# Loading keys a pair ahead of values in a single-core attention-decode kernel

## The chip, the core and the metric

The kernel runs on one core of one Trainium2 chip. The metric is the device time of one execution in microseconds (us): the median of three runs. TensorE (PE) multiplies matrices, VectorE (DVE) and ScalarE (ACT) do elementwise work, SyncE (SP) issues nearly all loads, and sixteen DMA engines carry them out.

## The reference

One new token attends to a cache of 65,536 tokens, with 16 query heads of width 256 that share 8 key/value heads in twos; a small mixer over the 448 model channels is blended in by a gate.

```python
g = sigmoid((x * gate_w).sum(-1))                 # x: 1 x 1 x 448
q = (x @ wq) as 16 heads of 256                   # k_cache, v_cache: 8 heads x 65536 x 256, bf16
scores = q . k * 256**-0.5                        # query heads 2g, 2g+1 use key/value head g
a = (softmax(scores) @ v) as one row of 4096 @ wo # 448 channels
h = layernorm(x)
b = gelu(h * w1 + b1) @ w2 + b2                   # per channel, through 1792 hidden units
out = g * a + (1 - g) * b
```

The two caches hold 537 MB, all of which is read once.

## The kernel before, in words

The work is cut into `NP` = 32 *pairs*, four (`PPH`) to each of `H` = 8 key/value heads. A pair is 16,384 cache rows: 128 rows (`NV`) of 256 values on each of 128 partitions, 8.39 MB of keys and as much of values. Its keys go through TensorE in eight chunks (`BODY`) of 16 rows (`NT`).

**Buffers.** `vbuf` holds the value rows of one pair. `kring` holds 192 rows: keys of an even pair stand in rows 0 to 127, those of an odd pair in rows 64 to 191. Both kinds of pair use the middle, rows 64 to 127, and every pair transposes the middle first (`tiles(HV)`, chunks 0 to 3), then its own side (`tiles(0)` or `tiles(NV)`). So the next pair's keys can be loaded when half of this pair's chunks are transposed.

**One pair on TensorE.** `keys`: each chunk is transposed into PSUM (`kst`, line 334); VectorE evacuates two of the four banks to `ktT` (line 616) and ScalarE the other two (line 751); then the scores against the two current queries `qcur` follow (line 353), one chunk behind the transposes. `values`: first `maxima`, a round trip in which VectorE reduces the scores (line 622), TensorE transposes (374) and spreads (376) the maximum, ScalarE makes the factor `fade` and the weights `pT` (734, 738), and VectorE scales the running sums in `acc` (645). Then TensorE adds the denominators (392) and multiplies the 128 value rows (403). In the first 14 pairs (`FT`), VectorE also does one step of the mixer after the maxima (`mixer`, lines 585 to 610) and TensorE adds its product (513).

**After four pairs**, the head ends: VectorE copies the sums (`take`, 650), TensorE clears `acc` and turns the head's output over partitions (`by_row`), VectorE scales it (676) and sets the next head's `qcur` (669), and TensorE projects it with this head's `wo` (450). The last head ends in `tail()`.

**The order of loads** is written out by hand in the SP queue: for each pair j, wait until half of pair j-1 is transposed, load keys j; wait until values j-1 are multiplied (`sem_pv`), load values j; once a head, wait for the projection and load the next `wo`. Everything else waits on the semaphores that these loads raise. Keys of pair 30 come in halves, of pair 31 in quarters, and the values of pair 31 as rows 0 to 95, 96 to 111, 112 to 123 and 124 to 127 (`pieces`), followed by the last head's `wo` in two halves. `spin` (line 369) multiplies without use, eight times before the last values and once in the tail.

Of the kernel before, what the change touches and what calls it, by code (L numbers as in the profile page):

```python
# [12 lines left out]
def bass_gated_mix__gqa_block_cached__mixer_token_mlp__decode_kernel(  # L13
# [17 lines left out]
    H = A_k_cache.shape[1]  # L31
# [4 lines left out]
    REP = HQ // H  # L36
# [27 lines left out]
    NFIRST = 96  # L64
    NLATE = 112
    pieces = [(NFIRST, NLATE), (NLATE, 124), (124, NV)]
# [16 lines left out]
    QV = NV // 4  # L83
# [10 lines left out]
    with ctx:  # L94
# [101 lines left out]
        sem_kp = new_sem("sem_kp")  # L196
        sem_kq = [new_sem("sem_kq%d" % i) for i in range(3)]
# [53 lines left out]
        @block.sync  # L251
        def _(eng):
            def load_wo(g):
                w = A_wo[g * REP * DH:(g + 1) * REP * DH, :]
                eng.dma_start(wo_rows, w.rearrange("(p i) n -> p (i n)", i=2 * REP)).then_inc(sem_wo, 16)

            load_wo(0)
            eng.dma_start(wq_a.rearrange("p j n -> p (j n)"),
                          A_wq[0:WF * P, :].rearrange("(p j) n -> p (j n)", p=P)).then_inc(sem_wq, 16)
            eng.dma_start(wq_b, A_wq[WF * P:DM, :].rearrange("r (a n) -> (r a) n", a=2)  # L260
                          ).then_inc(sem_wq, 16)
            def load(dst, cache, j, n0, n1, at, sem):
                eng.dma_start(dst[:, at + n0:at + n1, :].rearrange("p n d -> p (n d)"), src(cache, j, n0, n1)
                              ).then_inc(sem, 16)

            for j in range(NP):
                last = j == NP - 1
                if j >= 1:
                    eng.wait_ge(sem_tr[NB - 1], BODY * (j - 1) + DC)
                if j == 0:  # L270
                    load(kring, A_k_cache, j, HV, NV, 0, sem_k)
                    load(kring, A_k_cache, j, 0, HV, 0, sem_kb)
                elif last:
                    for i, sem in enumerate([sem_k] + sem_kq):
                        load(kring, A_k_cache, j, i * QV, (i + 1) * QV, HV, sem)
                elif j == NP - 2:
                    load(kring, A_k_cache, j, HV, NV, 0, sem_k)
                    load(kring, A_k_cache, j, 0, HV, 0, sem_kp)
                else:
                    load(kring, A_k_cache, j, 0, NV, HV * (j % 2), sem_k)  # L280
# [5 lines left out]
                load(vbuf, A_v_cache, j, 0, NFIRST if last else NV, 0, sem_v)  # L286
                if last:
                    for (n0, n1), sem in zip(pieces, sem_vp):
                        load(vbuf, A_v_cache, j, n0, n1, 0, sem)
                g, m = divmod(j, PPH)  # L290
                if m == 0 and 1 <= g < H - 1:
                    eng.wait_ge(s_proj, g)
                    load_wo(g)

            eng.wait_ge(s_proj, H - 1)
            for h in range(REP):
                w = A_wo[(HQ - REP + h) * DH:(HQ - REP + h + 1) * DH, :]
                eng.dma_start(wo_sb[:, h, :], w.rearrange("(p j) n -> p (j n)", j=2)).then_inc(sem_wl[h], 16)
            eng.wait_ge(s_fin, NCG)
            eng.dma_start(out_ap, out_row[:, :]).then_inc(sem_out, 16)  # L300
            eng.wait_ge(sem_out, 16)
# [13 lines left out]
        def _(pe):  # L315
# [3 lines left out]
            def transposes(k, c, j, u16, x2):  # L319
                if k == 0:  # L320
                    pe.wait_ge(sem_k, u16)
                if k == DC:
                    pe.wait_ge(sem_kb, 16)
                    with pe.If(j == NP - 2):
                        pe.wait_ge(sem_kp, 16)
                if k and k % (DC // 2) == 0:
                    with pe.If(j == NP - 1):
                        pe.wait_ge(sem_kq[k // (DC // 2) - 1], 16)
# [17 lines left out]
            def scores(k, c):  # L346
                par = k % 2
                for nt in range(NT):
# [10 lines left out]
            def keys(c0, *where):  # L359
                transposes(0, c0, *where)  # L360
                for k in range(1, BODY):
                    transposes(k, c0 + k, *where)
                    scores(k - 1, c0 + k - 1)
                scores(BODY - 1, c0 + BODY - 1)


            def spin(n):
                for _ in range(n):
                    pe.matmul(kst[:, NB - 1, :], ones_sq[:, :], ktT[:, KTB - 1, 0, 0:512], start=True, stop=True)  # L369
# [9 lines left out]
            def values(j, c0, u16):  # L379
                j1 = pe.snap(j + 1, min_val=1, max_val=NP)  # L380
                maxima(j1)
                with pe.If(j == NP - 1):
                    pe.wait_ge(s_mix, 1)
                    for q in range(NCG):
                        r = slice(32 * q, 32 * q + 1)
                        pe.matmul(prj[r, 0:WG], rest[r, :], brow[r, :], start=False, stop=True,
                                  skip_group_check=True)
                    spin(8)
                pe.wait_ge(s_acc, j1)
                pe.wait_ge(sem_exp, j1)  # L390
# [4 lines left out]
                def some(n0, n1, last=False):  # L395
                    if last:
                        piece_wait(n0)
                    else:
                        pe.wait_ge(sem_v, u16)
                    for n in range(n0, n1):  # L400
                        r, nt = divmod(n, NT)
                        o = 32 * (n % 4)
                        ins = pe.matmul(acc[o:o + REP, 0:DH], pT[:, r, 2 * nt:2 * nt + 2], vbuf[:, n, :],  # L403
                                        start=False, stop=False, skip_group_check=True)
                    return ins

                some(0, NFIRST)
                with pe.If(j < NP - 1):
                    some(NFIRST, NV).then_inc(sem_pv, 1)
                with pe.Else():  # L410
                    some(NFIRST, NLATE, last=True).then_inc(s_early, 1)
                    tail()
# [43 lines left out]
            def tail():  # L456
# [3 lines left out]
                spin(1)  # L460
# [40 lines left out]
            pe.reg_mov(x2_reg, 0)  # L501
            on = OrderedEngineSet([pe.engine])
            with nc.Fori(0, H, 1, engines=on, head_slot={pe.engine: 0}) as g:
                with nc.Fori(0, PPH, 1, engines=on, head_slot={pe.engine: 0}) as m:
                    j = pe.snap(g * PPH + m, min_val=0, max_val=NP - 1)
# [3 lines left out]
                    values(j, c0, u16)  # L509
                    with pe.If(j < FT):  # L510
                        pe.wait_ge(s_pb, j + 1)
# [3 lines left out]
                    pe.reg_sub(x2_reg, NV, x2_reg)  # L515
                with pe.If(g < H - 1):
                    pe.wait_ge(s_cp, g + 1)
                    clear(acc[:, 0:NACC])
                    by_row(acc[:, SELC:NACC]).then_inc(s_sel, 1)
                    pe.wait_ge(sem_wo, pe.snap(g * 16 + 16, min_val=16, max_val=16 * H))  # L520
                    pe.wait_ge(s_oTn, g + 1)
                    project(range(2 * REP)).then_inc(s_proj, 1)

        @block.vector
        def _(vec):
# [140 lines left out]
            def finish_head(g):  # L666
                take(vec.snap(g * PPH + PPH, min_val=PPH, max_val=NP))
                vec.memset(mrun[:, :], LOW)
                vec.tensor_copy(qcur[:, :, :], qT[:, :, bass.ds(g * REP + REP, REP)])
                vec.drain()  # L670
# [4 lines left out]
                vec.wait_ge(s_sel, g + 1)  # L675
# [5 lines left out]
            vec.tensor_copy(qcur[:, :, :], qT[:, :, 0:REP])  # L681
# [6 lines left out]
            with nc.Fori(0, H - 1, 1, engines=on) as g:  # L688
# [14 lines left out]
            with nc.Fori(NP - PPH, NP, 1, engines=on) as j:  # L703
                c0 = vec.snap(j * BODY, min_val=0, max_val=NC)
                for k in range(BODY):
                    evacuate(k, c0 + k)
                maxima(vec.snap(j + 1, min_val=1, max_val=NP), c0)
            take(1, s_early)
# [7 lines left out]
        def _(act):  # L716
# [5 lines left out]
            act.dma_start(b2_b[:, :], B_b2.rearrange("(a n) -> a n", a=1)).then_inc(sem_misc, 16)  # L722
            for b in range(1, NB, 2):
                act.sem_inc(sem_ev[b], 1)
# [63 lines left out]
```

## Time and profile before

| | |
|---|---|
| median of 3 runs | 1267.19 us (1265.81 to 1267.33) |
| profiled execution, its own time | 1267.84 us |
| span in the profile, first to last instruction | 1266.0 us |
| PE matmul busy | 976.4 us (77%) |
| PE weight load busy | 889.4 us (70%) |
| DVE / ACT busy | 498.6 us (39%) / 545.5 us (43%) |
| moved by DMA | 544.39 MB, mean 430 GB/s |
| mean granted TensorE clock | 0.852 of full speed |

The span is the time from the first to the last instruction in the trace; the execution's own time has 1.8 us around it. All times of instructions below are counted from the span's start. Busy shares are means over the whole span and do not tell which engine others wait for; the waits and the timeline do. "SPq" is the queue of SyncE that issues loads, "PEq" TensorE's sequencer. In the timeline a row gives start, duration, engine, line, operation, what is written and read, and how often.

### The profile page before, as it was taken

Reading aid. Unit: us, or ns where it says so; the run is one execution under the profiler, and the core shown is the slowest. Engines: PE = TensorE matmul, PEld = TensorE weight load, DVE = VectorE, ACT = ScalarE, POOL = GpSimd, SP = SyncE. Lnnn points to the kernel's source line nnn. Section 1 sums busy time; section 2 is a strip of 40 time slices with the busy share of each in tenths; the row PEclk is TensorE's granted clock in tenths of the full one; section 3 lists DMA queues with packets and bytes.
Section 4 is the critical chain, followed back from the end, with each engine's and each line's share of the span. In section 5 each row is a group of like instructions: output and inputs, shape, how many; then the busy total and the mean of one; then the engine's idle time right before and its main releaser. Section 6 shows DMA issues by size and latency. Waiting matters only on the chain.

```text
span 1266.0 us, 39302 instructions
## 1 busy us (share of the span) xinstructions
PE 976.4 (77%) x17210; PEld 889.4 (70%) x17210; DVE 498.6 (39%) x1125; ACT 545.5 (43%) x692; POOL 0.9 (0%) x7
## 2 busy tenths in 40 slices
PE   2877788777787777778687887778877787886888
PEld 2766678766687767677676876668777677776787
DVE  2434345344454444444233433324333334342443
ACT  0544345443355443454334543335443345433554
POOL 0000000000000000000000000000000000000000
PEclk9888788888888878888788898888877788887899
DMA  9999999999999999999999999999999999999998
GB/s 417 430 430 424 431 433 433 433 431 433 433 437 433 433 433 433 437 433 433 431 435 437 431 433 433 433 437 433 429 437 431 435 433 433 435 433 429 431 424 355
DMA packets 12056, 544.39 MB, mean 430 GB/s; under 512 B 1417, under 2 KB 1676, under 8 KB 2956
## 3 DMA queue, kind: packets, MB, share of 16 engines
q1 hardware_dynamic: 11954, 544.22, 99.6%
q8 instruction: 8, 0.13, 0.0%
q14 instruction: 4, 0.03, 0.0%
q10 hardware_dynamic: 90, 0.01, 0.0%
HBM read 544.22 MB, written 0.00 MB: 430 GB/s over the span
## 4 chain that ended last, share of the span: by engine, by line
DMA 66%; PE 32%; issue 1%; DVE 1%; SPq 0%; DVEq 0%
DMA kring<-in_A_k_cache_dram 66%; PE kst L334 25%; PE sps L353 5%; PE acc L403 1%; PE kst L369 0%; PE sps L376 0%; DVE mcol L622 0%; DVE acc L645 0%; PE acc L392 0%; PE sps L374 0%; DVE mrow L627 0%; PE sps L424 0%; DVE mdiag L629 0%; PE sps L431 0%; DVE mcol L625 0%
## 5 line engine op out<-in xcount | busy, mean ns | idle before, releaser
L751 ACT ACTIVATE ktT<-kst 128x1024 bf16<-128x1024 bf16 x512 | 499.7, 1023 | 555.7 <-PE kst L334 555.3
L334 PE MATMUL kst<-ident,kring 128*128 128x128 f32 x4096 | 555.4, 296 | 164.8 <-DMA kring<-in_A_k_cache_dram 144.7
L334 PEld LDWEIGHTS kst<-ident,kring 128*128 128x128 f32 x4096 | 504.5, 154 | 177.5 <-issue 174.6
L616 DVE COPY ktT<-kst 128x1024 bf16<-128x1024 bf16 x512 | 354.1, 692 | 606.9 <-PE kst L334 583.3
L353 PEld LDWEIGHTS sps<-qcur,ktT 128*128 128x128 bf16 x8192 | 237.8, 96 | 5.1 <-issue 2.6
L353 PE MATMUL sps<-qcur,ktT 128*128 128x2 bf16 x8192 | 236.7, 163 | 2.1 <-issue 2.1
L403 PE MATMUL acc<-vbuf,pT 128*2 128x256 bf16 x4080 | 177.2, 356 | 0.0
L403 PEld LDWEIGHTS acc<-vbuf,pT 128*2 128x2 bf16 x4080 | 116.5, 108 | 52.5
L392 PE MATMUL acc<-pT,ones_sq 128*128 128x32 bf16 x256 | 12.7, 190 | 51.0 <-DVE acc L645 51.0
L734 ACT ACTIVATE fade<-mdif 128x2 f32<-128x2 f32 x32 | 6.6, 205 | 95.5 <-DVE mdif L633 95.5
L392 PEld LDWEIGHTS acc<-pT,ones_sq 128*128 128x128 bf16 x256 | 9.5, 106 | 54.1 <-DVE acc L645 53.6
L376 PEld LDWEIGHTS sps<-mdiag,mones 2*128 2x128 f32 x64 | 13.7, 264 | 27.8 <-DVE mdiag L629 27.8
L376 PE MATMUL sps<-mdiag,mones 2*128 2x2 f32 x64 | 16.4, 324 | 21.2 <-DVE mdiag L629 21.2
L622 DVE TENSOR_REDUCE mcol<-sps 128x2 f32<-128x256 f32 x32 | 13.6, 424 | 44.4 <-PE sps L353 44.4
L738 ACT ACTIVATE pT<-sps,mneg 128x64 f32 x128 | 30.5, 336 | 0.0
L755 ACT ACTIVATE z_b<-z_b 128x448 bf16<-128x448 bf16 x14 | 8.1, 579 | 47.9 <-DVE z_b L603 47.9
L374 PE MATMUL sps<-ident,mcol 128*2 128x128 f32 x32 | 9.1, 283 | 24.1 <-DVE mcol L625 24.1
L374 PEld LDWEIGHTS sps<-ident,mcol 128*2 128x2 f32 x32 | 2.6, 80 | 26.9 <-DVE mcol L625 26.9
L645 DVE TENSOR_SCALAR acc<-acc,fader 128x256 f32<-128x256 f32 x32 | 15.8, 492 | 2.5
L650 DVE COPY accs<-acc 128x288 f32<-128x288 f32 x8 | 3.7, 458 | 32.8 <-PE acc L403 32.8
L627 DVE TENSOR_REDUCE mrow<-sps 2x1 f32<-2x128 f32 x32 | 8.9, 278 | 12.0 <-PE sps L374 12.0
L632 DVE TENSOR_SCALAR mneg<-sps 128x2 f32<-128x2 f32 x32 | 5.1, 159 | 19.4 <-PE sps L376 19.4
(108 smaller groups left out, 169.1 us busy)
## 6 DMA issues: line engine op xcount, KB each, us to landing
kring<-in_A_k_cache_dram SPq DMA_DIRECT2D x4, 4096.0 KB, 24.4
kring<-in_A_k_cache_dram SPq DMA_DIRECT2D x4, 2048.0 KB, 26.3
vbuf<-in_A_v_cache_dram SPq DMA_DIRECT2D x1, 6144.0 KB, 27.0
wo_sb<-in_A_wo_dram SPq DMA_DIRECT2D x7, 448.0 KB, 22.8
vbuf<-in_A_wq_dram SPq DMA_DIRECT2D x1, 3072.0 KB, 11.1
vbuf<-in_A_v_cache_dram SPq DMA_DIRECT2D x1, 1024.0 KB, 29.2
vbuf<-in_A_v_cache_dram SPq DMA_DIRECT2D x1, 768.0 KB, 30.6
vbuf<-in_A_wq_dram SPq DMA_DIRECT2D x1, 512.0 KB, 12.7
```

The costliest lines, as they stand in the source:

```text
L334: ins = pe.transpose(kst[:, b, i * P:(i + 1) * P], kring_f[:, at + NT * (k % DC) + 4 * b + i, :], ident[:, :])
L353: ins = pe.matmul(sps[:, 0, 2 * (NT * k + nt):2 * (NT * k + nt) + 2], ktT[:, par, b, ntl * DH + dj:(ntl + 1) * DH:2], qcur[:, dj, :], star ...
L374: pe.transpose(mxT, mcol[:, :], ident[:, :]).then_inc(s_mT, 1)
L376: pe.matmul(mxB, mones[:, :], mdiag[:, :], start=True, stop=True).then_inc(s_mB, 1)
L392: pe.matmul(acc[:, DENC:SELC], ones_sq[:, :], pT[:, r, :], start=False, stop=(r == BODY - 1), skip_group_check=True)
L403: ins = pe.matmul(acc[o:o + REP, 0:DH], pT[:, r, 2 * nt:2 * nt + 2], vbuf[:, n, :], start=False, stop=False, skip_group_check=True)
L616: vec.tensor_copy(ktT[:, k % KTB, b, :], kst_b[:, b, :]).then_inc(sem_ev[b], 1)
L622: vec.tensor_reduce(out=mcol[:, :], in_=scores_all.rearrange("p (n hh) -> p hh n", hh=REP), axis=AX.X, op=ALU.max)
L627: vec.tensor_reduce(out=mrow[:, :], in_=mxT, axis=AX.X, op=ALU.max)
L645: vec.tensor_scalar(acc[:, 0:DENC], acc[:, 0:DENC], fader[:, :], None, op0=ALU.mult).then_inc(s_acc, 1)
L738: ins = act.activation(pT[:, bass.ds(p0, DC), hh:2 * NT:REP], scores_all.rearrange("p (a r n hh) -> p a hh r n", a=2, r=DC, hh=REP)[:, hal ...
L751: act.activation(ktT[:, k % KTB, b, :], kst_b[:, b, :], AF.Copy).then_inc(sem_ev[b], 1)
```

## The change

Three things change together.

*Loads.* From pair 3 on, SP issues keys j before values j-1 (it was values j-1, then keys j). To get there, keys of pairs 2 and 3 are loaded in halves, each with a semaphore of its own where needed (`sem_kc`), and keys 30 and 31 are no longer cut. The last values come in five pieces. The first, 56 rows (`NRING`), goes into rows 0 to 55 of `kring`, which are free once all of pair 30 is transposed; the other 72 rows go to `vbuf`, after values 30.

*TensorE's loop.* One loop of 33 steps takes the place of the two nested loops. Step j does the maxima of pair j-1, the keys of pair j, the mixer's product, then the values of pair j-1. Steps 0 and 1 still do keys, maxima and values of the same pair, step 2 (`LEAD`) does keys alone, and step 32 has no keys. A head's end follows the values of its last pair, at the end of the next head's first step. The first scores of a step wait until ScalarE has read the scores of the pair before (`sem_exp`), and its keys until `qcur` is the right head's (`s_qc`). The spins are gone.

*VectorE.* It evacuates the first pair of the next head before it ends the head (`finish_head`), and sets `qcur` after the last maxima of a head.

The diff, cut to its core (SP, then TensorE, then VectorE):

```diff
-            for j in range(NP):
-                last = j == NP - 1
-                if j >= 1:
-                    eng.wait_ge(sem_tr[NB - 1], BODY * (j - 1) + DC)
...
-                elif last:
-                    for i, sem in enumerate([sem_k] + sem_kq):
-                        load(kring, A_k_cache, j, i * QV, (i + 1) * QV, HV, sem)
...
+            for j in range(NP):
+                if j == LEAD + 1:
+                    eng.wait_ge(sem_tr[NB - 1], BODY * LEAD)
+                    load(kring, A_k_cache, j, HV, NV, HV, sem_kc[1])
+                if j >= 1:
+                    eng.wait_ge(sem_tr[NB - 1], BODY * (j - 1) + DC)
+                if j == LEAD:
+                    load(kring, A_k_cache, j, HV, NV, 0, sem_k)
+                    load(kring, A_k_cache, j, 0, HV, 0, sem_kc[0])
+                elif j == LEAD + 1:
+                    load(kring, A_k_cache, j, 0, HV, HV, sem_k)
+                elif j >= 1:
+                    load(kring, A_k_cache, j, 0, NV, HV * (j % 2), sem_k)
+                if j < LEAD:
+                    load_v(j)
+                elif j > LEAD:
+                    load_v(j - 1)
+            for (n0, n1), sem in zip(pieces, sem_vp):
+                if n0 == 0:
+                    eng.wait_ge(sem_tr[NB - 1], BODY * (NP - 1))
+                elif n0 == NRING:
+                    eng.wait_ge(sem_pv, NP - 1)
+                load(kring if n1 <= NRING else vbuf, A_v_cache, NP - 1, n0, n1, 0, sem)
```

```diff
+            with nc.Fori(0, NP + 1, 1, engines=on, head_slot={pe.engine: 0}) as jj:
...
+                with pe.If(j > LEAD):
+                    maxima(pe.snap(j, min_val=1, max_val=NP))
+                with pe.If(j < NP):
...
+                    pe.wait_ge(s_qc, g)
+                    keys(c0, j, u16, pe.snap(x2_reg, min_val=0, max_val=NV))
+                with pe.Else():
+                    pe.wait_ge(s_mix, 1)
...
+                with pe.If(j < LEAD):
+                    maxima(pe.snap(j + 1, min_val=1, max_val=NP))
+                with pe.If(j != LEAD):
+                    values(j, pe.snap(v_reg, min_val=1, max_val=NP))
+                    pe.reg_add(v_reg, v_reg, 1)
+                with pe.If(m >= PPH):
+                    with pe.If(j < NP):
...
+                        project(range(2 * REP)).then_inc(s_proj, 1)
```

```diff
+            with nc.Fori(0, H, 1, engines=on) as g:
                 with nc.Fori(0, PPH, 1, engines=on) as m:
...
                     for k in range(BODY):
                         evacuate(k, c0 + k)
+                    with vec.If(j > 0):
+                        with vec.If(m < 1):
+                            finish_head(g)
                     maxima(vec.snap(j + 1, min_val=1, max_val=NP), c0)
                     with vec.If(j < FT):
                         mixer(j)
-                finish_head(g)
+                with vec.If(g < H - 1):
+                    vec.tensor_copy(qcur[:, :, :], ...).then_inc(s_qc, 1)
```

More of the change, by code (lines that the diff above doesn't have):

```diff
@@ L60, in bass_gated_mix__gqa_block_cached__mixer_token_mlp__decode_kernel @@
     HALF = NQ // 2
-    NFIRST = 96
+    LEAD = 2
+    assert LEAD % 2 == 0 and 1 < LEAD < PPH
     NLATE = 112
-    pieces = [(NFIRST, NLATE), (NLATE, 124), (124, NV)]
+    NRING = 56
+    pieces = [(0, NRING), (NRING, 96), (96, NLATE), (NLATE, 124), (124, NV)]
     NCG = 4
@@ L82, in bass_gated_mix__gqa_block_cached__mixer_token_mlp__decode_kernel @@
     HV = NV // 2
-    QV = NV // 4
     assert NP % 2 == 0
@@ L285, in _ @@
                     eng.wait_ge(sem_pv, j)
[L286 to L289, printed above, removed]
+                load(vbuf, A_v_cache, j, 0, NV, 0, sem_v)
                 g, m = divmod(j, PPH)
@@ L323, in transposes @@
                     pe.wait_ge(sem_kb, 16)
[L324 to L328, printed above, removed]
+                    for i, sem in enumerate(sem_kc):
+                        with pe.If(j == LEAD + i):
+                            pe.wait_ge(sem, 16)
                 def tiles(at):
@@ L357, in scores, with keys @@
                 ins.then_inc(sem_qk, 1)
-            def keys(c0, *where):
-                transposes(0, c0, *where)
+            def keys(c0, j, *where):
+                j1 = pe.snap(j + 1, min_val=1, max_val=NP)
+                transposes(0, c0, j, *where)
                 for k in range(1, BODY):
[L362 to L369, printed above, removed]
+                    transposes(k, c0 + k, j, *where)
+                    scores(k - 1, c0 + k - 1, j1)
+                scores(BODY - 1, c0 + BODY - 1, j1)
             def maxima(j1):
@@ L376, in maxima, with denominators @@
                 pe.matmul(mxB, mones[:, :], mdiag[:, :], start=True, stop=True).then_inc(s_mB, 1)
[L379 to L390, printed above, removed]
+            def denominators():
                 for r in range(BODY):
@@ L702, in _ @@
             vec.tensor_scalar(brow, brow1, bcast[:, 2:3], None, op0=ALU.add).then_inc(s_mix, 1)
[L703 to L708, printed above, removed]
+            take(NP, s_early)
             vec.wait_ge(s_late, 1)
```

116 lines of the change are left out of this document (69 added, 47 removed).

## The prediction

> **What bounds the kernel now.** I read the page's slices and queues first, then the waits of the queue that issues the loads, then the timeline and the landings of the last 60 us.
>
> ```profile
> DMA  9999999999999999999999999999999999999998
> GB/s 417 430 430 424 431 433 433 433 431 433 433 437 433 433 433 433 437 433 433 431 435 437 431 433 433 433 437 433 429 437 431 435 433 433 435 433 429 431 424 355
> ...
> q1 hardware_dynamic: 11954, 544.22, 99.6%
> ```
>
> The sixteen DMA engines are busy in every slice, and the load queue fills 99.6% of their span. Between 73.5 and 1164.8 us the windows give 433 GB/s without a break, so 8.39 MB (128 rows of keys or values) take 19.37 us and a pair 38.7. All 544 MB at that rate are 1257 us of the span of 1266.0. The page's chain names 66% DMA; the other third is work that hides a queue already full.
>
> ```profile
> SPq L263 <- PE acc L403: 680.9, 31, 24.8
> SPq L263 <- PE kst L334: 487.1, 31, 20.5
> ```
>
> These are the waits of the issuing queue, which let the next load go when a buffer is free. They cost nothing while an earlier load is still moving. An order matters only where the DMA engines run out, so I look for such places.
>
> ```profile
> 1224.79 5.21 PE L403 MATMUL acc<-vbuf,pT 128*2 128x256 bf16 x128
> 1230.06 1.75 SPq L263 DMA_DIRECT2D vbuf<-in_A_v_cache_dram  x4
> 1231.86 0.91 SPq L298 DMA_DIRECT2D wo_sb<-in_A_wo_dram  x2
> ...
> 1257.31 3.90 PE L403 MATMUL acc<-vbuf,pT 128*2 128x256 bf16 x112
> ...
> 1263.47 0.37 PE L450 MATMUL prj<-wo_sb,oTn 128*1 128x112 bf16 x16
> ...
> 1264.48 0.32 SPq L300 DMA_DIRECT2D out_dram<-out_row  x1
> ```
>
> This is the timeline of the end: start, duration, engine, line. Values of pair 30 finish at 1230.0, and that lets the last value rows go (1230.06, four pieces). With the landings below, the 96-row piece is in at 1257.1, the 16-row piece at 1259.6, the last output weights at 1263.2. TensorE ends its 112 rows at 1261.21, 1.6 us after the piece landed; the projection starts at 1263.47, 0.25 us after the last weights. From landing to the end of the span it is 1266.0 - 1263.2 = 2.8 us.
>
> ```profile
> vbuf<-in_A_v_cache_dram SPq DMA_DIRECT2D x1, 6144.0 KB, 27.0
> vbuf<-in_A_v_cache_dram SPq DMA_DIRECT2D x1, 1024.0 KB, 29.2
> ...
> wo_sb<-in_A_wo_dram SPq DMA_DIRECT2D x2, 224.0 KB, 30.9
> ```
>
> ```profile
> 1259.00:1260.00 1.00, 1.00 (x48) 0.82 (x40) 0.00 (x0) 0.00 (x0) 0.00 (x0) 1.00 0.98 366
> 1260.00:1261.00 1.00, 1.00 (x48) 0.76 (x36) 0.00 (x0) 0.00 (x0) 0.00 (x0) 1.00 0.81 299
> 1261.00:1262.00 1.00, 0.43 (x10) 0.22 (x2) 0.64 (x2) 0.00 (x0) 0.00 (x0) 1.00 0.26 95
> 1262.00:1263.00 1.00, 1.00 (x33) 1.00 (x33) 0.40 (x3) 0.00 (x0) 0.00 (x0) 1.00 0.05 18
> ```
>
> The windows (last two columns: DMA share, GB/s) show how the engines finish: 366, 299, 95, 18 GB/s. Not all stop together; a straggler works 1 to 2 us longer than the others. No byte moves after 1263.0, so a landing is told some 0.5 us after the last packet.
>
> **The change part by part.** The profiled execution took 1267.84 us with a span of 1266.0, 1.8 outside. The median shown, 1267.19, is 0.65 lower; I work in the span's clock and add the difference to the median.
>
> *The pairs in the middle: nothing.* Per step the queue still gets one 8.39 MB key load when half the pair before is transposed, and one value load when values are through. After: keys of pair j land at t; half are transposed at t+11 and the next keys go out, with value rows due until t+19.4, 8 us of cover. Keys are through at t+23.5, values (the pair before) at about t+28, and the next value load goes out 11 us before the keys moving then are in. The wait for the maxima (four engines' steps, 3.6 us, from L622 at 1220.81 to the end of L645 at 1224.42) leaves the path from keys to values; it goes into TensorE's wait for keys, 7.0 us before (1157.99 to 1164.95). The head's end (copy, clear, projection, 3 to 4 us) lies in that wait, as does the new wait for the next head's queries; behind it on TensorE is only that key pair, which isn't in yet.
>
> *One early place.* Pair 2 has no values behind it, so at pair 3 VectorE goes from the maxima into the mixer (L591 to L609, 139.16 to 143.52: 4.4 us) while keys wait to be evacuated. Counted on from the end of values 1 (106.8): keys 2 are through at 129, maxima at 133, the mixer at 137.5; only then are keys 3 (landed at 131.6) evacuated, half are through 10.5 later, and keys 4 move at 149. Values 2 last until 150.5: 1.5 us of cover. Without it this costs 0 to 2 us; I take 0.
>
> *Smaller pieces.* The quarters of the last key pair landed every 4.9 us where a quarter of 19.37 is 4.84; four such cuts go, one cut more of an early pair and one more of the values come: -0.2.
>
> *The last loads, the term that decides.* Before, 30's values and then 31's keys stood ahead of the last values. After, keys 31 land first: counted back from 1263.2 with weights 1.15, values 19.5, values 19.37 and the 0.2, at 1223.0. Values 30 (19.37) and 56 rows of values 31 (8.48) follow, 27.85 us of work. The queue runs dry with the straggler at 1250.4, with the others up to 2 us earlier. The other 72 rows wait for values 30, which now stand behind keys 31 on TensorE. Keys 31 start 0.1 after landing and take 23.4 from the first transpose to the last score (pair 28, 1125.33 to 1148.2, took 22.9; pair 29, 1164.95 to 1188.9, took 24.0): 1246.5. Then branches, 0.2 (a branch that drains TensorE shows as 0.3 to 0.4 "issue" in the chain, 0 when it is read ahead), and denominators, 0.35 (1224.48): 1247.05. Then 128 value matmuls. The two rows below are 3.0 us and 1.6 us of them:
>
> ```profile
> 1225.00:1228.00 3.00, 3.00 (x64) 1.93 (x60) 0.50 1.01 431
> 1228.10:1229.70 1.60, 1.60 (x68) 1.33 (x60) 1.00 1.03 440
> ```
>
> In the first the granted clock (third column from the end) is 0.50, in the second 1.00: four start every 0.21 us, then every 0.11. They began at half clock after 3.7 us without keys or values; directly behind scores at full clock they take 32 x 0.11 = 3.5, with three branches 3.8. The other bound is 5.5 (1152.45, 5.54). I take 3.8, as the windows keep 1.00 through the scores of pairs 29, 30 and 31 and 1.5 to 4 us beyond: 1250.85.
>
> The queue's issue comes 0.05 later (1230.01 to 1230.06), then the first bytes. The first load is issued at 0.74, and by 4.0 the windows (0, 55, 297, 477 GB/s) hold 1.9 us of full rate: 1.35 late. The output's store at 1264.48 moves after 1265.0: over 0.5. I take 1.0: 1251.9.
>
> [...]
>
> So the straggler idles 1251.9 - 1250.4 = 1.5 us, the others longer; all restart level. 72 rows are 10.9 us, weights 1.15, notice 0.5: landed at 1264.5, 1.3 later than before.
>
> *The tail.* The spins (L369) go; the copy of sums is earlier, so the first half of the projection is ready when the last weights land: -0.25 of 2.8 (0 to -0.6).
>
> Sum: 1264.5 + 2.55 = 1267.0 against 1266.0: **+1.0**, in the median 1268.2. A fresh measurement can tell about 0.2%, 2.5 us, from no change; this is under it.
>
> **The rivals.**
>
> *Never dry.* A quick pair 31 (22.6, the shortest in the trace) and first bytes in 0.5: the 72 rows move 1.3 us sooner, at 1250.6, as the straggler ends, and only -0.2 and -0.25 stay: 1266.7. Chance 0.12.
>
> *Late values, slower.* Place: the issue of the 72 rows, behind keys 31 and values 30. Keys 24.4, values 5.5 at half clock, branches 1.0: values 30 end 3.5 us after my 1250.85, and every microsecond of it is idle time for all sixteen engines: 1271.7. Decides where values 30 end later than 1252.4. For: the 5.5 us stretches, and a long wait ahead of keys that starts each pair cold. Against: nothing stands between scores and values any more. Chance 0.15.
>
> *Code fetched again, slower.* The loop body grows from some 1,450 to 1,530 TensorE instructions, weight loads counted. Before, the instruction queue q8 moved 8 packets, 0.13 MB, all before 80 us: the loop stays in place. If it no longer did, 6 or 7 packets of 16 KB in each of 33 steps, 0.6 us each at 433/16 GB/s, are 8 us if spread over the engines, 130 on one: 1275 or far more. Chance 0.04. [...]
>
> *Not what it says.* Keys "a pair ahead" are ahead of values only; their issue still hangs on half the pair before. I count that as the main case.
>
> *Faster by over 2.5 us* needs nearly the whole 2.8 behind the last landing, or a faster queue: 0.05, for what I don't see.
>
> **How the numbers follow.** Main case 0.64 at 1268.2, of it 0.04 beyond +2.5 (a dry place at pair 4 too). Same: 0.60 + 0.12 = 0.72; slower: 0.04 + 0.15 + 0.04 = 0.23; faster 0.05. The range goes from the never-dry case less 0.7 of scatter between runs (1265.81 to 1267.33) to near the late case, without the refetch: 1266.0 to 1270.9.
>
> **What would show it.** Right: 433 GB/s throughout, keys 31 landing near 1223, values 30 ending near 1251 with 0.11 us for four, a dip in GB/s of 1 to 3 us right after, the last weights near 1264.5. Wrong: no dip (never dry); a dip of 4 us or more, or one near 150 us; q8 packets after 80 us; key pairs further apart than 38.7 us.

## The result and the profile after

| | median | runs | ratio to before |
|---|---|---|---|
| before | 1266.84 us | 1265.75 to 1267.33 (7) | |
| after | 1274.37 us | 1272.94 to 1281.31 (7) | 1.0081, 95% interval 1.0054 to 1.0107 |

The changed kernel is slower, and above the predicted range (1266.0 to 1270.9). The ratio and its interval are worked out from all the runs; here and below they are not the quotient of the two medians. The runs of after fall into two groups with nothing in between: four at 1272.9 to 1274.4 us, three at 1280.6 to 1281.3. The profiled run is of the lower group (1272.94, span 1271.1, 1.8 around it as before). So two losses are to be found: the one that the lower group has to before (6.1 to 7.5 us against its median, 5.1 between the two profiled spans), and some 8 us between the groups.

The page of after, its slices and queues:

```profile
DMA  9999999999999999999999999999999999999996
GB/s 418 427 419 429 422 429 429 441 431 429 429 441 431 429 435 450 409 438 445 439 431 425 445 431 429 431 441 429 429 431 429 441 431 429 429 437 450 431 429 281
...
q1 hardware_dynamic: 11810, 544.22, 99.2%
q8 instruction: 8, 0.13, 0.0%
```

The load queue fills 99.2% of the engines' span, where it filled 99.6%. No slice of the middle is under 409; the last slice has 281 GB/s instead of 355. The instruction queue moves 8 packets, the last at 72.6 us: none came in the rest of the loop.

The end, from the timeline of after (start, duration, engine, line):

```profile
1248.05 0.36 PE L389 MATMUL acc<-pT,ones_sq 128*128 128x32 bf16 x8 [0.90 <-issue]
1248.34 5.33 PE L396 MATMUL acc<-vbuf,pT 128*2 128x256 bf16 x128
1253.71 1.85 SPq L264 DMA_DIRECT2D vbuf<-in_A_v_cache_dram  x4
...
1268.66 0.27 PE L457 MATMUL prj<-wo_sb,oTn 128*1 128x112 bf16 x8 [0.20 <-DMA wo_sb<-in_A_wo_dram]
```

and windows of the same stretch (the last three columns are granted clock, DMA share, GB/s):

```profile
1248.00:1249.00 1.00, 0.95 (x32) 0.84 (x36) 0.00 (x0) 0.00 (x0) 0.00 (x0) 0.97 1.07 459
1249.00:1250.00 1.00, 1.00 (x28) 0.70 (x20) 0.00 (x0) 0.00 (x0) 0.00 (x0) 0.50 0.07 29
...
1252.00:1253.00 1.00, 1.00 (x40) 0.81 (x32) 0.00 (x0) 0.00 (x0) 0.00 (x0) 0.82 0.00 0
1253.00:1254.00 1.00, 0.67 (x28) 0.33 (x16) 0.00 (x0) 0.00 (x0) 0.00 (x0) 1.00 0.00 0
1254.00:1255.00 1.00, 0.27 (x1) 0.08 (x1) 0.13 (x1) 0.00 (x0) 0.00 (x0) 1.00 0.78 184
```

Read them together. From 1249.1 to 1254.2 next to nothing moves: for five microseconds the DMA engines stand empty, nearly all of it until values 30 are multiplied. Their 128 matmuls end at 1253.67, and for 3.4 us of them the granted clock is 0.50 ("half clock" from here on). Then the last four pieces are issued; the last weights land at 1268.62 (before: 1263.2), and the rest of the tail is as predicted.

The second place is early. Windows of after around the load of keys 4:

```profile
146.50:150.00 3.50, 3.09 (x64) 2.99 (x61) 1.38 (x2) 2.67 (x3) 0.00 (x0) 1.00 1.08 393
150.00:152.00 2.00, 2.00 (x31) 1.99 (x30) 1.28 (x2) 0.97 (x2) 0.00 (x0) 1.00 0.28 98
```

Keys 4 go out at 148.7, 1.4 us before the load ahead of them ends, and still the engines run dry: keys 4 land at 171.24, 1.8 us later than 19.36 behind values 2 (150.1).

### The profile page after: what moved, and what is told of

Its sections match the earlier page's. It is cut to its first block, busy times and chain, and to the rows that moved or that the text cites. A ratio compares the mean times of both kernels' runs of the same rounds, so it can differ in the third digit from the quotient of the medians.

```text
span 1271.1 us, 39820 instructions
## 1 busy us (share of the span) xinstructions
PE 964.5 (76%) x17201; PEld 887.8 (70%) x17201; DVE 497.3 (39%) x1125; ACT 544.5 (43%) x692; POOL 0.9 (0%) x7
## 3 DMA queue, kind: packets, MB, share of 16 engines
q1 hardware_dynamic: 11810, 544.22, 99.2%
## 4 chain that ended last, share of the span: by engine, by line
DMA 58%; PE 37%; DVE 2%; issue 2%; DVEq 1%; SPq 0%; ACT 0%
DMA kring<-in_A_k_cache_dram 57%; PE kst L344 27%; PE sps L365 7%; PE acc L396 2%; DMA wo_sb<-in_A_wo_dram 1%; PE acc L446 0%; ACT z_b L791 0%; PE sps L384 0%; PE acc L389 0%; DVE ktT L650 0%; DVE z_b L631 0%; DVE z_b L635 0%; DVE wtmp L629 0%; DVEq L624 0%; SPq L264 0%
## 5 line engine op out<-in xcount | busy, mean ns | idle before, releaser
L344 PE MATMUL kst<-ident,kring 128*128 128x128 f32 x4096 | 563.6, 299 | 200.7 <-DMA kring<-in_A_k_cache_dram 169.3
L344 PEld LDWEIGHTS kst<-ident,kring 128*128 128x128 f32 x4096 | 511.4, 155 | 209.3 <-issue 200.2
L396 PE MATMUL acc<-vbuf,pT 128*2 128x256 bf16 x4024 | 161.1, 336 | 3.7 <-issue 2.3
L396 PEld LDWEIGHTS acc<-vbuf,pT 128*2 128x2 bf16 x4024 | 112.3, 102 | 44.2 <-issue 4.7
L384 PEld LDWEIGHTS sps<-mdiag,mones 2*128 2x128 f32 x64 | 10.9, 211 | 27.9 <-DVE mdiag L663 27.9
L389 PE MATMUL acc<-pT,ones_sq 128*128 128x32 bf16 x256 | 11.9, 181 | 24.1 <-issue 20.7
L384 PE MATMUL sps<-mdiag,mones 2*128 2x2 f32 x64 | 13.6, 280 | 21.3 <-DVE mdiag L663 21.3
L389 PEld LDWEIGHTS acc<-pT,ones_sq 128*128 128x128 bf16 x256 | 8.7, 99 | 27.4 <-issue 23.8
L679 DVE TENSOR_SCALAR acc<-acc,fader 128x256 f32<-128x256 f32 x32 | 15.8, 492 | 2.5
```

Of the source, the lines that this page charges most:

```text
L344: ins = pe.transpose(kst[:, b, i * P:(i + 1) * P], kring_f[:, at + NT * (k % DC) + 4 * b + i, :], ident[:, :])
L384: pe.matmul(mxB, mones[:, :], mdiag[:, :], start=True, stop=True).then_inc(s_mB, 1)
L389: pe.matmul(acc[:, DENC:SELC], ones_sq[:, :], pT[:, r, :], start=False, stop=(r == BODY - 1), skip_group_check=True)
L679: vec.tensor_scalar(acc[:, 0:DENC], acc[:, 0:DENC], fader[:, :], None, op0=ALU.mult).then_inc(s_acc, 1)
```

## The experiments

Every run was measured beside before, which had a median of 1266.15 us for `a1` and `e1` to `e3`, 1266.87 for `e4` to `e6` and `b1`, and 1266.66 for `e7` to `e9` and `b2`. One run of each was profiled.

Four theories were tested: the end is set by when the last 72 rows are let go (A); the mixer's step stands between values and keys in the early pairs and makes the two groups (B); the clock of values 30 (C); code fetched again or the key ring as such (D, the rivals).

### The last loads alone (A), and the changed kernel once more

`a1_again` is the changed kernel without an edit.

> The changed kernel once more, to see which of its two groups of times (1273 to 1274, and 1281) a run falls in, and to have a trace of the upper group. If the early place is what differs (keys 4 issued after values 2 are in), keys 4 land 9 to 10 us after values 2 plus 19.4 in an upper run, 1.8 in a lower one. If the end differs, keys 31 land near 1223 in both and the last rows start 7 us later. If the queue is slower throughout, key pairs stand further apart than 38.7 us.

Measured: 1280.58 us (four runs: 1273.81, 1279.09, 1282.07, 1283.04), ratio 1.0121 (1.0104 to 1.0138). One run lies in the lower group; the others lie high, at 1279.1 to 1283.0, more widely than before. The profiled run is the lowest (1273.81): its keys 4 land 1.6 us later than 19.36 behind the load ahead, near the 1.8 that was expected of a lower run. It is no trace of the upper group.

`e1_rows72_first`: rows 56 to 127 of every pair are multiplied first, so that the room of the last 72 rows is free 56 matmuls sooner.

```diff
-                    eng.wait_ge(sem_pv, NP - 1)
+                    eng.wait_ge(s_72, NP - 1)
...
-                    some(NLATE, NV, vbuf).then_inc(sem_pv, 1)
+                    some(NLATE, NV, vbuf).then_inc(s_72, 1)
+                    some(0, NRING, vbuf).then_inc(sem_pv, 1)
```

> Values 56 to 127 of a pair are multiplied before values 0 to 55, and the last 72 rows' load waits for those alone. Theory of the late values: the load goes out some 2.0 us earlier (72 of 128 rows at mixed clock), the sixteen engines idle 2.0 less, and the time falls by 2.0. Rival that the end hangs on something else (the ramp after the idle time, the tail): 0. The upper group, if it comes from the early place, stays.

Measured: 1283.92 us (1277.57 to 1285.31), ratio 1.0127 (1.0098 to 1.0156). By the total this fails, as 2.0 less was expected. The trace splits it: from keys 31's landing to the last landing it is 1279.04 - 1234.82 = 44.2 us, against 45.5 (after) and 45.8 (`a1_again`). So the end gained 1.3 to 1.6, but keys 31 landed 11 us later, an upper-group start in the profile, and three of four times lie high. As a total it decides nothing.

`e3_ring64`: 64 rows instead of 56 in the key ring (`NRING = 64`), so 8 rows less behind the restart.

> 64 instead of 56 of the last rows go to the key ring. Theory of the late values: the restart comes at the same time with 64 rows left instead of 72, 1.2 us less: -1.2. Rival, the last 56 rows in the ring are themselves late for TensorE: 0 or slower.

Measured: 1272.27 us, ratio 1.0067 (1.0040 to 1.0094); four runs at 1271.0 to 1272.3, three at 1280.2 to 1280.8. Against before the lower group came down by 1.1 (from 6.7 to 5.6 above it, in medians), the upper did not (14.2 and 14.5), and the two groups stay. From keys 31 (1231.72) to the last landing (1275.94) it is 44.2: that is 1.3 less than in after, the 8 rows' own 1.2 us, as the theory of the dry queue has it. The profile is of the upper group, and shows where that loses.

### The mixer between values and keys (B)

Timeline of `e3_ring64` at pair 6, whose values 4 end at 252.85 (PE and DVE rows):

```profile
255.93 1.96 PE L344 MATMUL kst<-ident,kring 128*128 128x128 f32 x16 [0.89 <-DMA kring<-in_A_k_cache_dram]
...
256.82 0.34 DVE L625 TENSOR_SCALAR wtmp<-hbT,params 128x448 bf16<-128x448 bf16 x1 [0.18 <-issue]
...
260.79 0.39 DVE L643 TENSOR_TENSOR gu<-wtmp,z_b 128x448 bf16<-128x448 bf16 x1
261.51 1.29 DVE L650 COPY ktT<-kst 128x1024 bf16<-128x1024 bf16 x2 [0.32 <-issue]
262.25 3.68 PE L344 MATMUL kst<-ident,kring 128*128 128x128 f32 x16 [4.36 <-DVE ktT L650]
...
266.62 3.65 PE L344 MATMUL kst<-ident,kring 128*128 128x128 f32 x16
...
274.65 0.33 SPq L264 DMA_DIRECT2D kring<-in_A_k_cache_dram  x1
```

The keys are there at 255.8, and TensorE transposes the first chunk. Then it stands for 4.36 us, because the bank that it needs is emptied by VectorE, and VectorE does the maxima of pair 5 and then the mixer (L625 to L643) before it evacuates. When it goes on, sixteen transposes take 3.65 us instead of 1.95: half clock, for several chunks. Half the pair is transposed 18.7 us after its start instead of 11 to 11.5, the next keys are issued at 274.65, and the value load ahead of them ends at 275.1. That is the cover used up.

The clock stays low for different times in the profiles. Windows at pair 3, first of after (lower group), then of `e3_ring64` (upper), then of `a1_again` (lower):

```profile
143.10:146.50 3.40, 3.40 (x76) 3.38 (x75) 1.97 (x3) 2.34 (x4) 0.00 (x0) 1.00 1.07 463
```

```profile
143.10:146.50 3.40, 3.40 (x45) 3.40 (x44) 0.75 (x2) 1.50 (x2) 0.00 (x0) 0.50 0.80 347
146.50:150.00 3.50, 3.50 (x46) 3.44 (x45) 1.17 (x2) 1.57 (x2) 0.00 (x0) 0.50 0.43 187
150.00:152.00 2.00, 2.00 (x17) 1.94 (x16) 0.91 (x2) 1.02 (x1) 0.00 (x0) 0.50 0.00 0
```

```profile
143.10:146.50 3.40, 3.40 (x34) 3.40 (x32) 0.89 (x2) 1.72 (x2) 0.00 (x0) 0.50 0.85 366
146.50:150.00 3.50, 3.50 (x68) 3.43 (x67) 1.83 (x3) 2.08 (x4) 0.00 (x0) 0.82 0.35 150
```

After the wait for VectorE the records of the granted clock show half clock from 139.62 to 143.03 in after, 3.41 us, and from 138.57 to 152.23 in `e3_ring64`, 13.66 us. Half of pair 3 is done after 15.8 us in the one, 19.7 in the other.

That alone does not make the group. `a1_again`, a lower run, has half clock from 130.71 to 147.78 (17.07 us), and 17.9 us for half of pair 3. `e1_rows72_first`, an upper run, has it for 3.42 (140.74 to 144.16) and 15.8 us, like after. The four profiles part at pair 5: half of it takes 16.8 and 17.7 us in the two lower ones, and keys 6 are issued 3.5 and 2.6 us before the load ahead of them lands; it takes 19.7 in both upper ones, and keys 6 are issued 0.4 and 0.6 us after. From there the upper ones stay late: half of pair 6 takes 18.7 and 19.0 us, against 11.7 and 11.6.

In `e3_ring64` three key loads start at an empty or nearly empty queue: keys 4 land 4.55 us later than 19.36 behind the load ahead, keys 6 2.8 later, keys 7 2.2 later; with 1.1 from two value loads that is 11 us. In after only the 1.8 at keys 4 are lost. The difference, 9 us, is about the distance of the groups; keys 31 land at 1231.72 and 1223.13. In `e1_rows72_first` it is 1.2 at keys 4, then 3.0, 2.2, 2.1 and 1.8 at keys 6, 7, 8 and 10. Why the clock stays low for 3.4 us in one run and for 13.7 or 17.1 in another was not settled.

`e2_no_mixer` leaves the fourteen steps of the mixer out on VectorE, ScalarE and TensorE (the output lacks that part).

> The mixer's 14 steps on VectorE, ScalarE and TensorE are left out (the output lacks that part). Theory of the early place: keys 4 are issued some 4 us earlier, before the queue runs dry; the lower group falls by 1.8 or less, and the upper group (1281) disappears. Rival, the upper group comes from the end or from a slower queue: it stays.

Measured: 1271.03 us (1269.19 to 1271.7, six runs), ratio 1.0034 (1.0021 to 1.0046). One group. Keys 4 land 19.36 behind values 2 to 0.01 us, keys 31 at 1221.28, 1.85 sooner than in after.

`e4_mixer_beside` keeps the work and moves it: one step of the mixer in pairs 3 to 16, on VectorE between the evacuation of a pair's keys and its maxima, where it waits for nothing that the next keys need.

```diff
+                    with vec.If(j > LEAD):
+                        with vec.If(j < LEAD + 1 + FT):
+                            mixer(vec.snap(j, min_val=1, max_val=NP))
...
                     maxima(vec.snap(j + 1, min_val=1, max_val=NP), c0)
-                    with vec.If(j < FT):
-                        mixer(j)
```

> Nothing is left out: the 14 mixer steps move from pairs 0 to 13 to pairs 3 to 16, and on VectorE and ScalarE they stand before the maxima, beside TensorE's values, instead of between the maxima and the next keys. Theory of the closed loop (values, maxima, mixer, keys in a row leave a step no slack against 38.7 us of loads): the upper group disappears and the time is that of the kernel without mixer, 1269 to 1272. Rival, the mixer costs wherever it stands (VectorE's share, its drains): the upper group stays.

Measured: 1270.02 us (1268.99 to 1272.58, ten runs), ratio 1.0024 (1.0014 to 1.0034), one group. Windows of this kernel at the place that ran dry in after:

```profile
143.10:146.50 3.40, 2.99 (x59) 2.88 (x58) 1.63 (x3) 2.19 (x3) 0.00 (x0) 1.00 1.02 443
146.50:150.00 3.50, 3.50 (x79) 3.41 (x76) 1.61 (x3) 2.75 (x4) 0.00 (x0) 1.00 1.04 449
150.00:152.00 2.00, 2.00 (x34) 1.99 (x33) 1.38 (x2) 1.35 (x3) 0.00 (x0) 1.00 1.13 492
```

No dip. Pairs 3 and 5 take 24.1 and 23.3 us from the first transpose to the last score, where after took 28.3 and 29.3. Theory B holds: without the mixer, or with it elsewhere, none of 16 runs is in the upper group and the 1.8 us of the lower one are gone, so the mixer's place makes both. What is left to before, 3.2 us, is the end: from keys 4 to keys 31 no key load lands late.

### The end, step by step

`e5_staged` is `e4_mixer_beside` with values multiplied as rows 56 to 95, 96 to 127, 0 to 55, and each of the first two stretches lets its own loads go.

```diff
-                    eng.wait_ge(sem_pv, NP - 1)
+                    eng.wait_ge(s_r1, NP - 1)
+                elif n0 == 96:
+                    eng.wait_ge(s_r2, NP - 1)
```

> The kernel before in this call, and values are multiplied in the order 56 to 95, 96 to 127, 0 to 55; the load of rows 56 to 95 waits for the first 40 alone, the rest for the next 32. Theory of the late values: the load goes out some 3.7 us earlier, about when the queue runs dry; idle time (3.3) and ramp (1.3) go nearly whole, time 1266.5 to 1267.5, as before the change. Rival, the ramp belongs to small pieces and not to idle engines: only 2 to 3 us less, 1268 to 1269.

Measured: 1269.26 us (1268.33 to 1270.61), ratio 1.0019 (1.0010 to 1.0029). Keys 31 to last landing: 1263.57 - 1222.28 = 41.3 us, against 44.7 in `e4_mixer_beside`; of the 3.4 won, 0.76 arrive in the median. The last instruction is now 4.4 us behind the last landing instead of 2.5. The time is a miss: 1266.5 to 1267.5 was expected. The loads were no longer last; TensorE was. And the restart was not free: the rows were issued 1.4 us before the load ahead of them landed, and landed 1.2 late.

`e6_staged64` adds the 64 rows of `e3_ring64`.

> The staged kernel with 64 rows in the key ring. Theory of the late values: the queue is already fed in time, so 8 rows more bring 0 to 0.5 us. If the queue still runs dry in the staged kernel: 1.2 less.

Measured: 1269.8 us (1268.66 to 1270.45), ratio 1.0020 (1.0011 to 1.0030): nothing, within what was expected. From keys 31 to the last landing it is 41.6 us, against 41.3 in `e5_staged`. Its timeline shows what is last:

```profile
1252.95 0.27 PE L386 MATMUL sps<-ident,mcol 128*2 128x128 f32 x1 [1.25 <-issue]
1253.89 0.38 PE L388 MATMUL sps<-mdiag,mones 2*128 2x2 f32 x2 [0.67 <-DVE mdiag L668]
1256.61 0.21 PE L535 MATMUL prj<-z_b,rest 1*1 1x112 bf16 x4 [2.34 <-DVE z_b L748]
1257.19 0.39 PE L393 MATMUL acc<-pT,ones_sq 128*128 128x32 bf16 x8 [0.37 <-issue]
1257.51 3.38 PE L400 MATMUL acc<-kring,pT 128*2 128x256 bf16 x64
```

Between values 30 (to 1251.70) and the ring's rows (1257.51) lie branches, the maxima, and a wait of 2.34 for the row that the mixer adds; and the 64 rows run at half clock, 53 ns each.

`e7_mix_early` makes that row before pair 31 is evacuated.

```diff
+                    with vec.If(j == NP - 1):
+                        vec.wait_ge(s_proj, H - 1)
+                        vec.tensor_copy(brow1, prj[:, WG:2 * WG])
...
+                        vec.tensor_scalar(brow, brow1, bcast[:, 2:3], None, op0=ALU.add).then_inc(s_mix, 1)
                     for k in range(BODY):
                         evacuate(k, c0 + k)
```

> The staged version with the ring of 64 rows (1269.8 us), with one move: VectorE makes the row that the mixer adds (three small operations) before it evacuates the keys of pair 31, and no longer after the last maxima. In the staged version the denominators of pair 31 began at 1257.19, behind the product with that row at 1256.61, though the weights were written at 1255.6 and the sums scaled at 1255.85. Theory (the end is bound by TensorE and VectorE between values 30 and the last values): denominators at about 1256.1, end 1.1 us earlier, 1268.7 us, and the last instruction 3.1 us after the last landing (was 4.2). Rival (the end is bound by the last landing): no change, 1269.8 us.

Measured: 1268.56 us (1267.15 to 1270.13), ratio 1.0017 (1.0007 to 1.0026): 1.2 less, near the theory's 1.1; against before it is 1.0 less (1.9 above it instead of 2.9), and the two intervals overlap, so the gain in time is likely and not shown. In the profile the stretch from the end of values 30 to the denominators shrinks from 5.49 to 4.25 us. The tail behind the last landing did not shrink in the profiled run (4.4 us): its last 128 rows took 5.5 us instead of 4.7, more of them at half clock. The shorter stretch is shown, the predicted tail isn't.

`e8_mix_spin` adds six useless 128x512 multiplications (`spin`) there.

```diff
                         pe.matmul(prj[r, 0:WG], rest[r, :], brow[r, :], start=False, stop=True,
                                   skip_group_check=True)
+                    spin(6)
```

> The version before it, with six useless 128x512 multiplications on TensorE between the last maxima and the last denominators. Theory (the clock stands at 0.5 there because TensorE has little to do): the 64 ring rows, 3.38 us in the staged version, take about 1.7; the loads then bind the end again at about 1262.8 + 2.5 us of tail: 1267.2 us. Rival (the clock stays at 0.5 whatever is put there): the six take 2.6 us instead of 1.3, outlast the wait for the weights by up to 1 us, the rows still take 3.4, and the time is 1269 us or more.

Measured: 1267.96 us (1265.48 to 1269.1, ten runs), ratio 1.0012 (1.0002 to 1.0022). The profiled run is its fastest, 1265.48, with a span of 1263.7:

```profile
1252.99 1.24 PE L386 MATMUL kst<-ktT,ones_sq 128*128 128x512 bf16 x5 [0.16 <-issue]
1254.41 0.36 PE L398 MATMUL acc<-pT,ones_sq 128*128 128x32 bf16 x8 [0.18 <-DVE acc L690]
1254.70 1.92 PE L405 MATMUL acc<-kring,pT 128*2 128x256 bf16 x64
1256.44 1.05 PE L405 MATMUL acc<-vbuf,pT 128*2 128x256 bf16 x32
1257.73 0.61 PE L405 MATMUL acc<-vbuf,pT 128*2 128x256 bf16 x16 [0.24 <-DMA vbuf<-in_A_v_cache_dram]
```

The 64 rows take 1.92 instead of 3.38, and the last rows wait for their loads again (0.24, the last row): the loads bind the end, the last landing is at 1261.20, 40.2 us behind keys 31, and the tail 2.5. The median came down by 0.6 of the 1.4 expected, and the intervals overlap here too. This version is the changed order with most of its losses mended, and stands 0.12% behind before (0.02 to 0.22), not ahead of it.

### The clock of values 30 (C)

`e9_spin_keys` puts four such multiplications behind the last scores of every pair of `e4_mixer_beside`.

> The version with the mixer beside the evacuation (1270.02 us), with four useless 128x512 multiplications on TensorE after the last scores of every pair, ahead of the denominators. Theory (values 30 take 5.33 us and not 3.8 because the clock falls in the gap of some 1.2 us behind the scores): values 30 in about 3.8 us, the last loads and the end up to 1.5 us earlier less what the four cost beyond the gap (0 to 0.5 us): 1268.5 to 1269.0 us. Rival (the pace is set by the matmuls before, or by something other than that gap): values 30 still 5.3 us and the four add up to 1 us: 1270 to 1271 us.

Measured: 1268.82 us (1267.67 to 1271.11), ratio 1.0018 (1.0008 to 1.0028). Timeline of the place:

```profile
1243.86 0.81 PE L383 MATMUL kst<-ktT,ones_sq 128*128 128x512 bf16 x3
1244.50 0.35 PE L395 MATMUL acc<-pT,ones_sq 128*128 128x32 bf16 x8
1244.79 3.67 PE L402 MATMUL acc<-vbuf,pT 128*2 128x256 bf16 x128
```

3.67 us instead of 5.33, and so in every pair from 2 to 30; without the four, 8 of these 29 pairs have it. The four cost 0.2 us a pair between the last score and the denominators: 0.7, where 0.5 of "issue" stood without them. Values 30 end at 1248.45 (1251.06 without them), and the last landing comes 2.5 sooner in the profiled run, the fastest of its ten. The median is 1.0 nearer to before than that of `e4_mixer_beside`, with overlapping intervals: the clock is shown, the gain in time is likely.

### The ring alone (D)

`b1_ring_only` is the kernel before, with its order, and only the 56 rows put into the key ring; its loop then holds the 56 value matmuls twice.

```diff
-                some(0, NFIRST)
+                with pe.If(j < NP - 1):
+                    some(0, NRING)
+                with pe.Else():
+                    some(0, NRING, buf=kring)
+                some(NRING, NFIRST)
```

> The kernel before the change with one part of it alone: the first 56 of the last 128 value rows go to the key ring, as soon as pair 30 is transposed. The queue holds 31's keys then and never ran dry, so all theories that put the loss into a dry queue expect no change (0, at most -0.3 at TensorE's end). If the pieces or the ring cost by themselves: slower by 1 or more.

Measured: 1313.32 us (1293.68 to 1328.11), ratio 1.0406 (1.0343 to 1.0469). A miss by 46 us. Its page:

```profile
GB/s 416 424 429 434 440 421 375 328 455 422 422 341 357 432 444 422 436 432 444 418 440 424 440 430 428 440 428 432 432 428 434 434 436 424 426 446 426 422 430 367
...
q8 instruction: 27, 0.44, 0.2%
```

The instruction queue moves 27 packets of 16 KB instead of 8. Eighteen of them come in two bursts of nine, from 190 to 237 us and from 358 to 407, right behind the ends of heads 0 and 1, and the slices there fall to 328 and 341 GB/s. The six large loads in and behind these bursts land 26 us late in sum, and this profiled run, the fastest of the four (1293.68), is 27 us above before.

`b2_ring_short` keeps the ring and moves the last pieces and the tail, some 70 matmuls, behind the loops.

```diff
-                with pe.Else():
-                    some(NFIRST, NLATE, last=True).then_inc(s_early, 1)
-                    tail()
...
+            some(NFIRST, NLATE, last=True).then_inc(s_early, 1)
+            tail()
```

> The kernel before with 56 of the last 128 value rows in the key ring, as in the run that took 1313 us, but with the last value pieces and the tail moved behind TensorE's loops, so that the loops hold about as many instructions as in the kernel before. Theory (the loss of 46 us came from TensorE's code being fetched again in every pass of the outer loop): the instruction queue moves 8 packets again, no slice below 400 GB/s in mid-span, 1265 to 1269 us. Rival (the ring piece or the branch between two copies of the value rows costs the time): 1300 us or more, as before.

Measured: 1266.71 us (1265.98 to 1268.19) against 1266.66, ratio 1.0003 (0.9994 to 1.0013), with

```profile
q8 instruction: 9, 0.15, 0.0%
```

(eight before 108 us, one at 1262.8 for the tail). The ring costs nothing that these runs can tell; the loss was code, fetched again (27 packets against 9). The expectation above speaks of every pass of the outer loop, the trace of the profiled run shows two passes. Why only two passes fetch is not shown.

## Why the prediction was wrong

Its sum against the profiled run of after, in the span's clock:

| step | predicted | measured |
|---|---|---|
| keys 31 landed | 1223.0 | 1223.13 |
| keys 31 on TensorE | 23.4 | 23.9, to 1247.14 |
| branches and denominators | 0.55 | 1.2 |
| values 30 | 3.8, to 1250.85 | 5.33, to 1253.67 |
| from there to the last landing | 13.65 | 14.95, to 1268.62 |
| tail | 2.55 | 2.48 |
| span | 1267.0 | 1271.1 |

**Values 30.** The step that failed is "I take 3.8, as the windows keep 1.00 through the scores ... and 1.5 to 4 us beyond". The clock fell to 0.5 at 1248.95, 1.8 us behind the last score, for 3.41 us. That is 1.5 us, and its bound (5.5) stood in the text. The windows cited were of the order before, and even they spoke against 3.8: the clock had to hold for 0.55 + 3.8 = 4.35 us behind the scores, and "1.5 to 4 us beyond" is shorter. In after, 25 of the 29 value groups of pairs 2 to 30 take 5.0 to 5.3 us. That multiplying without use in the gap behind the scores kept the clock is shown by `e9_spin_keys` (1.00 from 1245 to 1248, 3.67 us). Why the clock fell with 0.9 us of issue gap is not shown.

**Branches.** Taken as 0.2, they were 0.90 of "issue" ahead of L389; with the denominators that is 0.65 more. TensorE has several conditions between the last score and the denominators. No row shows why a branch should take 0 in one place and 0.3 to 0.4 in another: before has 0.31 and 0.42 of "issue" at two of them (1177.37, 1230.42).

**Restart.** "I take 1.0" for the first bytes; the windows 1254 and 1255 hold 184 and 164 GB/s, and against 12.05 us of work and 0.5 of notice the stretch to the last landing is 2.4 longer, 1.35 more than taken. With all sixteen engines empty the queue did not come back at full rate at once: 430 GB/s stand first in the window 1256.

With keys 31 through 0.65 later than forecast these are 0.65 + 0.65 + 1.5 + 1.3 = 4.1: the whole difference between the predicted span and that of the profiled run, which is of the lower group. It is the rival "Late values, slower", past its point of decision (1252.4) at 1253.67; it had 0.15, and should have been the main case, as the two ends of "values" were 3.5 and 5.5 and only rows from another order spoke for the lower. Its time, 1271.7, lay above the range given, and it had no term for the slower restart.

**One early place.** The cover of 1.5 us was right in its times (keys 4 issued at 148.7, predicted 149). "I take 0" was wrong: a load issued 1.4 us ahead of the end of the last one came 1.8 late, so a cover of 1.5 us was not enough here.

**The pairs in the middle: nothing.** This step made the upper group. It placed the head's end and the maxima in TensorE's wait for keys, and counted the mixer only once, at pair 3. But VectorE does maxima, mixer, evacuation in that order in every one of the first fourteen pairs: 3.6 us of maxima, 4.4 of mixer, 23 of keys, 1.2 of branches and denominators and 5.3 of values are 37.5 of the 38.7 us that a pair's loads take. A chunk at half clock takes 1.7 us more, and then the round is longer than the loads: at pair 6 of `e3_ring64` it is 40.4 us from the end of values 4 to the end of values 5 (252.85 to 293.28). Elsewhere the step held: in after no load between keys 4 and keys 31 lands more than 0.1 us late. No case of the prediction had two groups.

**What held.** 433 GB/s in the middle, the tail to 0.1, no code fetched again, and the place of the loss: a dip behind the last full loads. That keys 31 land to 0.1 us where they were forecast is luck: with 1.8 us lost at keys 4 they land at 1223.13, without that loss (`e2_no_mixer`, `e4_mixer_beside`) at 1221.3 and 1221.2, so the 1223.0 was 1.8 too late and the loss taken as 0 made up for it. "Code fetched again" was priced at 8 us or more and 0.04. It did not happen here, and happened with 56 more matmuls in the kernel before. Its 6 or 7 packets a step were an estimate that no run shows; `b1_ring_only` shows two bursts of nine.

**Against before.** Before let the last rows go 33 us ahead of the last landing; the new order brings keys ahead of values, and so puts the last value rows behind a full pair of keys on TensorE: 15 us ahead. With the five edits of `e4` to `e8` it comes to 0.12% behind before.

## What to carry over

A queue that is full 99.6% of its time has little to win: ask of a new order of loads where the queue will run dry, at the first pair and at the last, and take the slow end for every step behind an empty queue, the clock above all. List for each engine the order of its work in the new loop and add up the whole round; where it comes near the period of the loads, the cover that a single step shows is not there. When a loop's code grows, look at the packets of the instruction queue.

## What the runs showed that was not expected

- TensorE's clock fell to half with 0.9 us of gap behind matmuls of two columns, for 3.41 us; four 128x512 multiplications in the gap kept it in every pair (128 values in 3.67 instead of 5.33 us).
- Two groups of times, 8 us apart, came from an order without slack: 2 to 3 us more at pair 5 put the next key load behind the end of the queue, and the delay stayed. The length of half clock at pair 3 does not tell the group. With slack (`e4_mixer_beside`) there is one group.
- A loop some 115 TensorE instructions longer, of about 1,570 (counted from the kernel's text), fetched nine packets of 16 KB twice in the profiled run; the four runs lost 27 to 61 us. The changed kernel's loop of about 1,530 fetched none after 72.6 us. Whether the length makes the difference, or the nesting of the loops, stays open.
- A key load issued into an empty queue came 2.4 us late (`e1_rows72_first`, `e3_ring64`). Those issued 0.9 to 2.4 us before the load ahead of them landed still came 0.9 to 1.8 late (`a1_again`, after, `e1` and `e5` to `e7`); one issued 3.1 us before came 0.1 late (`e8_mix_spin`).
